# Chunk-selecting attention with a mixture of experts: score units of seven tiles, and another split of work in the first five pairs

## The chip, the cores and the metric

The kernel runs on one core of a Trainium2 chip, in one launch. The metric is the device time of one execution in microseconds (us). The engines are TensorE (PE; PEld is its weight load), VectorE (DVE), ScalarE (ACT) and GpSimd (POOL); SyncE (SP) only issues transfers here.

## The reference

The first half is attention in which each query sees only six chunks of 32 keys; the second half is a dense layer plus one routed expert of eight.

```python
# q, k, v: (4, 8, 768, 64); chunks of 32 keys
k_min, k_max = np.min(k_chunks, axis=3), np.max(k_chunks, axis=3)
ub = np.sum(np.maximum(q * k_min, q * k_max), axis=-1)       # per query and chunk
ub = np.where(causal, ub, -1e9)
top_chunks = np.argsort(ub, axis=-1)[..., -6:]
mask = sel & (pos[:, None] >= pos[None, :])                  # chosen chunk, and not later
scores = np.where(mask, q @ k.T / sqrt(64), -1e9)
attn_out = softmax(scores) @ v
x = attn_out.transpose(0, 2, 1, 3).reshape(3072, 512)
y_dense = np.maximum(x @ w1_dense, 0) @ w2_dense
# expert e = argmax(x @ w_gate), with its softmax weight
y_moe[rows of e] = gate_w * (np.maximum(x[rows of e] @ w1[e], 0) @ w2[e])
return y_dense + y_moe
```

## The kernel before

There are four batches of eight heads. The kernel takes two heads (g = 0 and 1) of a batch as one **pair**: the two heads' 64 features fill the 128 partitions. There are 16 pairs, four to a batch. A head has 768 positions, six tiles of 128. Scores are kept transposed (keys on the partitions, queries on the columns), so the causal half of a head is 21 tiles of 128 x 128.

**Preparation of a pair** is spread over the two pairs before it. `cast_qk` and `cast_v` turn the loaded fp32 values into fp16 on POOL. `prep_k` transposes the keys on PE into `pk`; ACT copies them to `kp`; DVE reduces `kp` to the largest and smallest key of each chunk (`ks`, line 502) and multiplies them by a sign mask into `kb` (line 505). `prep_kt` copies each half of `kp` into the key operand of its head, `kT[..][0]` and `kT[..][1]` (lines 509 and 510). `prep_q` transposes the queries into `pq`; ACT takes their relu into `qp` (line 520), DVE their negation into the query operands `rT` (lines 521 and 522). `prep_ub` makes the bounds `ub` on PE, and DVE finds the sixth largest of each query (`MAX8`, line 538) and flags the chunks below it (`fl`, line 540). `prep_s` transposes the flags on PE and DVE copies them into the free half of `rT` (lines 548 and 549). The free half of `kT` holds `exf`, a table of 30000 in the rows that belong to a key's chunk: so the score matmul itself adds the mask of unchosen chunks. `expand` copies `exf` into the six key operands once. There are three sets of `kT`, `rT` and `v16` (`NB` = 3), used in turn.

**A unit** is one score tile, `sp`, with its exp, `ex`. `scores` does the score matmuls (line 560) and the exp on ACT (line 564); where the unit lies on the diagonal, POOL zeroes the later keys in place (`affine_select`, line 566). `av` then multiplies `ex` with the values (line 579) into the output bank `op`, where a column of ones gives the row sum. After the last unit of a head `norm` takes the reciprocal (line 588) and writes the normalised rows to `xbig` (line 590). A pair has eleven units of up to four tiles (512 columns, one PSUM bank): five for each head, and one that holds the last two diagonal tiles of both. There are three score banks, two output banks (so one head's output can begin while the other's is normalised), and three banks for everything else. There are six `ex` tiles in SBUF.

**Order.** The loop runs over all 16 x 11 units. At step i it issues the scores of unit i + 2, then pieces of other work, then `av` of unit i - 1. The pieces stand at fixed units of a pair: flags of the next pair at unit 2, keys, queries, key operands and bounds of the pair after it at 4, 5, 7 and 9, casts and loads at units 0 and 7. An `issue_after` puts a piece behind the newest scores on PE and behind the exp before them on ACT. From the fifth pair on `fills` adds the work of the batch before: transposes of `xbig`, the gate, ranks, the scatter of rows to a table in DRAM (`place`), and 28 pieces of the dense layer (lines 387, 390, 399 and 404). `route_consts` makes the routing constants on POOL and writes empty rows to the table (line 187); it runs in the third pair. Expert weights are loaded by POOL's queue, one or two matrices a pair (line 206).

After the last pair the dense layer of the last batch and the expert blocks follow: rows are fetched from the table, multiplied with an expert's weights and added to the output by POOL's indirect transfers (line 744).

## Time and profile before

| what | value |
|---|---|
| median of three runs | 258.7 us (255.52 to 258.92) |
| the profiled execution | 257.3 us, span 255.5 us |
| mean granted TensorE clock | 0.994 |
| busy PE, DVE, ACT, POOL | 214.3, 179.8, 175.6, 159.6 us |
| first exp of the first pair | at 17.19 us |
| sixth pair begins, attention ends | at 55.13 us, at about 166.8 us |
| DMA packets | 75124, 50.12 MB |

The profile is of one execution. A row of the timeline gives the start from the begin of the span, the time that the instruction or merged run of instructions took, engine, line and operation; in brackets stands idle time ahead of it and what ended it. An instruction's own time includes its latency, so instructions that follow one another on an engine overlap a little: the time from start to start is what one costs an engine that is busy without a break. The busy share of PE is modelled from the starts of its matmuls.

### The profile page before, as it was taken

The numbers are of one execution on the slowest core, as the hardware profiler recorded it, in microseconds if no ns is written. First come the engines' busy times: TensorE is split into PE (matmuls) and PEld (weight loads), VectorE is DVE, ScalarE is ACT, GpSimd is POOL, SyncE is SP. The second block draws the span as 40 slices with busy tenths as digits, with TensorE's granted clock in tenths as the row PEclk, the third lists the DMA queues.
The fourth block names the chain that finished last, engine by engine and source line by source line (L and its number), as shares of the span: only waits on it lengthen the run. The fifth ranks groups of instructions, "written<-read, shape, count | busy, mean of one in ns | idle before, by whom it ended". The sixth has DMA issues, their size and how long they took to land. (4 is left out here: it accounts for less than half of the span.)

```text
span 255.5 us, 7236 instructions
## 1 busy us (share of the span) xinstructions
PE 214.3 (84%) x2547; PEld 141.4 (55%) x2547; DVE 179.8 (70%) x558; ACT 175.6 (69%) x332; POOL 159.6 (62%) x198
## 2 busy tenths in 40 slices
PE   1378969887989989999989988989579999999970
PEld 0256746655657676766567755655235555555530
DVE  6869989999989699898698896267233345555540
ACT  2799979877779887889789778924346465555530
POOL 4746998566177984379997235515755366776871
PEclk9999999999999999999999999999999999999997
DMA  7999999999889799979999934356979999885884
GB/s 179 262 266 236 213 225 264 228 210 209 215 146 323 122 293 247 232 164 212 321 213 270 198 76 129 106 152 193 249 164 206 232 220 186 144 140 70 120 122 92
DMA packets 75124, 50.12 MB, mean 196 GB/s; under 512 B 29648, under 2 KB 68176, under 8 KB 75088
## 3 DMA queue, kind: packets, MB, share of 16 engines
q1 hardware_dynamic: 59856, 30.33, 46.5%
q0 software_dynamic: 15232, 19.32, 46.1%
q8 instruction: 21, 0.34, 0.5%
q14 instruction: 15, 0.12, 0.2%
HBM read 41.93 MB, written 18.23 MB: 235 GB/s over the span
## 5 line engine op out<-in xcount | busy, mean ns | idle before, releaser
L564 ACT ACTIVATE ex<-sp 128x512 f16<-128x512 f32 (+1 forms) x176 | 91.3, 607 | 8.4 <-PE sp L560 4.1
L560 PE MATMUL sp<-rT,kT 128*128 128x128 f16 (+3 forms) x384 | 65.4, 260 | 3.9 <-ACT ex L564 2.4
L744 POOL DMA_INDIRECT out_dram<-yo,xg x28 | 43.2, 1545 | 23.5 <-DVE yo L743 17.2
L566 POOL TENSOR_SCALAR_AFFINE_SELECT ex<-ex 128x512 f16<-128x512 f16 x48 | 32.1, 683 | 39.7 <-ACT ex L564 28.9
L579 PE MATMUL op<-v,ex 128*128 128x65 f16 x672 | 48.5, 194 | 1.9 <-POOL ex L566 1.2
L579 PEld LDWEIGHTS <-ex 128*128 128x128 f16 x672 | 37.9, 98 | 20.3 <-POOL ex L566 5.7
L743 DVE TENSOR_SCALAR yo<-yp,xg 128x512 f32<-128x512 f32 x27 | 20.3, 751 | 24.0 <-PE yp L736 12.5
L370 POOL DMA_INDIRECT table<-xbig,slot x24 | 23.9, 997 | 19.1 <-issue 13.7
L560 PEld LDWEIGHTS <-kT 128*128 128x128 f16 x384 | 29.0, 98 | 8.5 <-issue 5.4
L718 ACT COPY ehT<-tp 128x512 f16<-128x512 f16 x28 | 16.4, 585 | 24.0 <-PE tp L716 17.3
L736 PE MATMUL yp<-we,ehT 128*128 x112 | 28.9, 379 | 2.1 <-ACT ys L404 1.3
L502 DVE TENSOR_REDUCE ks<-kp 128x24 f16<-128x768 f16 x30 | 27.3, 943 | 4.7 <-ACT kp L491 4.6
L387 PE MATMUL hp<-xT,wd 128*128 128x384 f16 x128 | 29.0, 325 | 1.5 <-DVE xT L258 1.3
L707 PE MATMUL hp<-we,exT 128*128 x112 | 29.1, 379 | 1.0 <-DVE exT L701 1.0
L399 PE MATMUL yp<-wd,hT 128*128 128x512 f16 x96 | 25.3, 379 | 2.8 <-issue 2.8
L710 ACT ACTIVATE eh<-hp 128x512 f16<-128x512 f32 x28 | 16.7, 597 | 12.4 <-PE hp L707 10.5
L701 DVE COPY exT<-tp 128x512 f16<-128x512 f16 x28 | 11.8, 423 | 15.7 <-PE tp L699 6.7
L390 ACT ACTIVATE hT<-hp 128x384 f16<-128x384 f32 x32 | 16.0, 502 | 8.8 <-PE hp L387 7.2
L491 ACT COPY kp<-pk 128x768 f16<-128x768 f16 x16 | 12.9, 806 | 9.1 <-PE pk L489 8.8
L404 ACT COPY ys<-yp 128x512 f32<-128x512 f32 x24 | 14.6, 607 | 6.4 <-PE yp L399 3.5
L590 DVE TENSOR_TENSOR xbig<-op,rs 128x384 f16<-128x384 f32 x32 | 17.5, 547 | 0.2
L736 PEld LDWEIGHTS <-ehT 128*128 128x128 f16 x112 | 10.1, 98 | 10.5 <-issue 1.7
(127 smaller groups left out, 383.1 us busy)
## 6 DMA issues: line engine op xcount, KB each, us to landing
we<-in_moe_w_dram POOLq DMA_DIRECT2D x16, 512.0 KB
kf<-in_k_dram SPq DMA_DIRECT2D x32, 192.0 KB
qf<-in_q_dram SPq DMA_DIRECT2D x32, 192.0 KB
vf<-in_v_dram SPq DMA_DIRECT2D x32, 192.0 KB
out_dram<-ys SPq DMA_DIRECT2D x48, 128.0 KB
xg<-table SPq DMA_DIRECT2D x28, 136.0 KB
table<-zt SPq DMA_DIRECT2D x9, 136.0 KB
wd<-in_moe_w_dense_dram POOLq DMA_DIRECT2D x2, 512.0 KB
```

Of the source, the lines that this page charges most:

```text
L370: sc = nc.gpsimd.indirect_dma_start(out=table, out_offset=bass.IndirectOffsetOnAxis(ap=keep["slot"][:, t : t + 1], axis=0), in_=xbig[b % 2 ...
L387: nc.tensor.matmul(hp, wd[:, ko, j * 128 : (j + 1) * 128], xT[:, ko, g * G * 128 : (g + 1) * G * 128], start=(ko == 0), stop=(ko == NK - 1))
L399: nc.tensor.matmul(yp, hold["h"][:, j, i * 128 : (i + 1) * 128], wd[:, NK + j], start=(j == 0), stop=(j == NK - 1))
L502: nc.vector.tensor_reduce(out=ks[:, i], in_=kp.rearrange("d (c w) -> d c w", w=32), op=op, axis=mybir.AxisListType.X)
L560: last = nc.tensor.matmul(sp[:, o : o + w], kT[p % NB][g][:, kt * 128 : (kt + 1) * 128], rT[p % NB][g][:, a * 128 : z * 128], start=(o == ...
L564: scored.append((last, nc.scalar.activation(ex[:, 0:o], sp[:, 0:o], AF.Exp, scale=-0.125)))
L566: latest["pool"] = nc.gpsimd.affine_select(out=ex, in_=ex, compare_op=ALU.is_ge, fill=0.0, base=0, pattern=[[0, 4], [1, 2], [2, 64]], chan ...
L579: nc.tensor.matmul(s["op", g][:, t * (D + 1) : (t + 1) * (D + 1)], ex[:, o : o + 128], v16[p % NB][:, g, kt, :], start=first, stop=(last_o ...
L707: nc.tensor.matmul(hp, s["xT"][:, ko], wef[:, bass.ds(offs[i] + ko * 512, 512)], start=(ko == 0), stop=(ko == NK - 1))
L736: nc.tensor.matmul(yp, s["hT"][:, j], wef[:, bass.ds(offs[i] + (NK + j) * 512, 512)], start=(j == 0), stop=(j == NK - 1))
L743: nc.vector.tensor_scalar(o, yp, gate, None, ALU.mult)
L744: sc = nc.gpsimd.indirect_dma_start(out=out, out_offset=to, in_=o, in_offset=None, bounds_check=N - 1, oob_is_err=False, compute_op=ALU.by ...
```

## The change

A head now has three units of seven tiles (896 columns over two PSUM banks): the first holds its six diagonal tiles and one other, so a pair has six units and two of them are masked. There are two score tiles of two banks, one output bank instead of two, and five `ex` tiles. `av` of a diagonal unit comes two steps after it instead of one, and the next unit's with it. The pieces stand in twelve slots of a pair, two a step.

In the first five pairs (`LEAN` = 5) the causal mask is added in PSUM by two matmuls of the identity with a constant tile, `later`, ahead of the score matmuls, and there is no `affine_select`. The keys of these pairs are copied by ACT straight into `kT[..][1]`. For the second to fifth pair POOL copies head 0's half from there to `kT[..][0]`, writes the `exf` rows over it, copies head 0's negated queries from `rT[..][1]` to `rT[..][0]`, and multiplies `kb`; DVE takes the relu in ACT's place. In the later pairs, and nearly so in the first, this preparation stays as it was, but `rT[..][1]` is now the whole negation and `rT[..][0]` its half. `route_consts` moves from the third to the fifth pair.

```diff
...
                                 fill=-60000.0, base=j, pattern=[[128, NT], [0, 2], [-32, NC]], channel_multiplier=2)
     for i in range(NB):
         nc.vector.memset(kT[i][0][64:128], 0.0)
-        nc.vector.memset(kT[i][1][0:64], 0.0)
         nc.vector.memset(v16[i][:, :, :, D : D + 1], 1.0)
 
     def members():
...
         nc.gpsimd.affine_select(out=exf[0:32], in_=exf[0:32], compare_op=ALU.is_ge, fill=0.0,
                                 base=31, pattern=[[-1, S]], channel_multiplier=32)
 
+
+    LEAN = 5
+    later = acst.tile([128, 128], HF)
+    nc.vector.memset(later, 0.0)
+    nc.gpsimd.affine_select(out=later, in_=later, compare_op=ALU.is_ge, fill=30000.0, base=0,
+                            pattern=[[1, NJ], [NJ, 64]], channel_multiplier=-1)
+
     def expand(i):
         nc.scalar.copy(kT[i][0][64:96, :], exf[0:32])
-        nc.scalar.copy(kT[i][1][0:32, :], exf[0:32])
 
 
     iom8 = const.tile([128, NT, E], FP)
...
 
     def of(g):
         return [
-            [(g, i, i, i + 1) for i in range(4)],
-            [(g, 0, 1, 5)],
-            [(g, 1, 2, 6)],
-            [(g, 2, 3, 6), (g, 4, 5, 6)],
-            [(g, 3, 4, 6), (g, 0, 5, 6)],
+            [(g, 0, 0, 1), (g, 1, 1, 2), (g, 2, 2, 3), (g, 3, 3, 4), (g, 5, 5, 6), (g, 4, 4, 6)],
+            [(g, 0, 1, 5), (g, 0, 5, 6), (g, 3, 4, 6)],
+            [(g, 1, 2, 6), (g, 2, 3, 6)],
         ]
 
-    units = of(0) + [[(g, i, i, i + 1) for g in range(2) for i in (4, 5)]] + of(1)
+    units = of(0) + of(1)
+    UW = 7 * 128
     NU = len(units)
     last_of = {}
     first_of = {}
     for u, pc in enumerate(units):
         for g, kt, a, z in pc:
-            first_of.setdefault(g, (u, kt))
             for t in range(a, z):
+                first_of.setdefault(g, (u, kt, t))
                 last_of[g, t] = (u, kt)
     done = [max(last_of[g, t][0] for t in range(NT)) for g in range(2)]
 
...
         at.setdefault(15, []).append(ranks)
         for t in range(NT):
             at.setdefault(18 + 4 * t, []).append(place(t))
-        U = HP * NU
+        U = 2 * HP * NU
         for n, f in enumerate(dense):
             at.setdefault(7 + n * (U - 9) // len(dense), []).append(f)
         return out_list, dense, ranks, [place(t) for t in range(NT)], at
...
     FIRST = 6
     with (
         tc.tile_pool(name="ahead", bufs=2) as ahead,
-        tc.tile_pool(name="aexp", bufs=6) as aexp,
-        tc.tile_pool(name="psc", bufs=3, space=bass.MemoryType.PSUM) as psc,
-        tc.tile_pool(name="pout", bufs=2, space=bass.MemoryType.PSUM) as pout,
+        tc.tile_pool(name="aexp", bufs=5) as aexp,
+        tc.tile_pool(name="psc", bufs=2, space=bass.MemoryType.PSUM) as psc,
+        tc.tile_pool(name="pout", bufs=1, space=bass.MemoryType.PSUM) as pout,
         tc.tile_pool(name="pprep", bufs=3, space=bass.MemoryType.PSUM) as pprep,
     ):
         def cast_qk(p):
...
             pk = pprep.tile([128, S], HF, name="pk", tag="pp")
             for t in range(NT):
                 nc.tensor.transpose(pk[:, t * 128 : (t + 1) * 128], s["k16"][:, t].rearrange("p g d -> p (g d)"), ident)
-            s["kp"] = kp = ahead.tile([128, S], HF, name="kp")
+            s["kp"] = kp = kT[p % NB][1] if p < LEAN else ahead.tile([128, S], HF, name="kp")
             nc.scalar.copy(kp.rearrange("d (T p j) -> d T p j", p=128, j=NJ),
                            pk.rearrange("d (T j p) -> d T p j", p=128, j=NJ))
             ks = ahead.tile([128, 2, NC], HF, name="ks")
...
                     nc.vector.tensor_reduce(out=ks[:, i], in_=kp.rearrange("d (c w) -> d c w", w=32), op=op,
                                             axis=mybir.AxisListType.X)
             s["kb"] = kb = ahead.tile([128, 2, 2, NC], HF, name="kb")
-            nc.vector.tensor_tensor(kb, ks.unsqueeze(2).to_broadcast([128, 2, 2, NC]), hmask, ALU.mult)
+            (nc.gpsimd if 0 < p < LEAN else nc.vector).tensor_tensor(kb, ks.unsqueeze(2).to_broadcast([128, 2, 2, NC]), hmask, ALU.mult)
 
         def prep_kt(p):
             kp = st[p]["kp"]
-            nc.vector.tensor_copy(kT[p % NB][0][0:64], kp[0:64])
-            nc.vector.tensor_copy(kT[p % NB][1][64:128], kp[64:128])
+            k0, k1 = kT[p % NB]
+            if p >= LEAN:
+                nc.vector.tensor_copy(k0[0:64], kp[0:64])
+                nc.vector.tensor_copy(k1[64:128], kp[64:128])
+            elif p:
+                nc.gpsimd.tensor_copy(k0[0:64], k1[0:64])
+                latest["pool"] = nc.gpsimd.tensor_copy(k1[0:32], exf[0:32])
+            else:
+                nc.vector.tensor_copy(k0[0:64], k1[0:64])
+                nc.scalar.copy(k1[0:32], exf[0:32])
 
         def prep_q(p):
             s = st[p]
...
                 nc.tensor.transpose(pqv[:, t // NJ, :, t % NJ], s["q16"][:, t].rearrange("p g d -> p (g d)"), ident)
             s["qp"] = qp = ahead.tile([128, S], HF, name="qp")
             r0, r1 = rT[p % NB]
-            nc.scalar.activation(qp, pq, AF.Relu)
-            nc.vector.tensor_single_scalar(r0, pq, -1.0, ALU.mult)
-            nc.vector.tensor_single_scalar(r1[64:128], pq[64:128], -1.0, ALU.mult)
+            if 0 < p < LEAN:
+                nc.vector.tensor_single_scalar(r1, pq, -1.0, ALU.mult)
+                nc.vector.tensor_single_scalar(qp, pq, 0.0, ALU.max)
+                latest["pool"] = nc.gpsimd.tensor_copy(r0[0:64], r1[0:64])
+            else:
+                nc.scalar.activation(qp, pq, AF.Relu)
+                nc.vector.tensor_single_scalar(r1, pq, -1.0, ALU.mult)
+                nc.vector.tensor_single_scalar(r0[0:64], pq[0:64], -1.0, ALU.mult)
 
         def prep_ub(p):
 
...
             nc.tensor.matmul(ub.rearrange("p t g c -> p (t g c)"), ident, cbias.rearrange("p t g c -> p (t g c)"),
                              start=True, stop=False, skip_group_check=True)
             for t in range(NT):
-                for n, (src, j) in enumerate(((s["qp"], 0), (s["qp"], 1), (rT[p % NB][0], 1))):
+                for n, (src, j) in enumerate(((s["qp"], 0), (s["qp"], 1), (rT[p % NB][1], 1))):
                     nc.tensor.matmul(ub[:, t].rearrange("p g c -> p (g c)"), src[:, t * 128 : (t + 1) * 128],
                                      s["kb"][:, j].rearrange("p g c -> p (g c)"),
                                      start=False, stop=(n == 2), skip_group_check=True)
...
 
         scored = []
 
+        def diagonal(u):
+            return units[u][0][1] == units[u][0][2]
+
         def scores(p, u):
             s = st[p]
             pc = units[u]
-            sp = psc.tile([128, 512], FP, name="sp")
+            sp = psc.tile([128, 1024], FP, name="sp")
+            o = 0
+            masked = p < LEAN and diagonal(u)
+            for n in (4, NT - 4) if masked else ():
+                nc.tensor.matmul(sp[:, o : o + n * 128].rearrange("p (n k) -> p n k", k=128), ident,
+                                 later.unsqueeze(1).to_broadcast([128, n, 128]),
+                                 start=True, stop=False, skip_group_check=True)
+                o = 512
             o = 0
             for g, kt, a, z in pc:
                 w = (z - a) * 128
                 last = nc.tensor.matmul(sp[:, o : o + w], kT[p % NB][g][:, kt * 128 : (kt + 1) * 128],
-                                 rT[p % NB][g][:, a * 128 : z * 128], start=(o == 0), stop=True, skip_group_check=True)
+                                 rT[p % NB][g][:, a * 128 : z * 128], start=(o % 512 == 0 and not masked), stop=True, skip_group_check=True)
                 o += w
-            ex = aexp.tile([128, 512], HF, name="ex")
-            scored.append((last, nc.scalar.activation(ex[:, 0:o], sp[:, 0:o], AF.Exp, scale=-0.125)))
-            if pc[0][1] == pc[0][2]:
-                latest["pool"] = nc.gpsimd.affine_select(out=ex, in_=ex, compare_op=ALU.is_ge, fill=0.0, base=0,
-                                        pattern=[[0, 4], [1, 2], [2, 64]], channel_multiplier=-1)
+            ex = aexp.tile([128, UW], HF, name="ex")
+            scored.append((last, nc.scalar.activation(ex, sp[:, 0:UW], AF.Exp, scale=-0.125)))
+            if diagonal(u) and not masked:
+                dg = ex[:, 0 : NT * 128]
+                latest["pool"] = nc.gpsimd.affine_select(out=dg, in_=dg, compare_op=ALU.is_ge, fill=0.0, base=0,
+                                        pattern=[[0, NT], [1, 2], [2, 64]], channel_multiplier=-1)
             s["ex", u] = ex
 
         def av(p, u):
...
             o = 0
             for g, kt, a, z in units[u]:
                 for t in range(a, z):
-                    first = first_of[g] == (u, kt) and t == a
+                    first = first_of[g] == (u, kt, t)
                     if first:
                         s["op", g] = pout.tile([128, 512], FP, name="op")
                     nc.tensor.matmul(s["op", g][:, t * (D + 1) : (t + 1) * (D + 1)], ex[:, o : o + 128],
...
 
         wq = [(e, w) for e in range(E) for w in range(2)]
         ahead_n = 2
-        LAG = 1
 
         def finish(p, u):
             av(p, u)
...
                     fills.update(batch_fills(p // HP)[-1])
 
         seq = [(p, u) for p in range(NP) for u in range(NU)]
+        due = {}
+        at = 0
+        for i, (p, u) in enumerate(seq):
+            at = max(at, i + (2 if diagonal(u) else 1))
+            due.setdefault(at, []).append((p, u))
         for i in range(ahead_n):
             scores(*seq[i])
-        for i, (p, u) in enumerate(seq):
+
+        def pieces(i, p, slot):
             n1 = p + 1 if p + 1 < NP else None
             n2 = p + 2 if p + 2 < NP else None
-            if i + ahead_n < len(seq):
-                scores(*seq[i + ahead_n])
 
             with tc.issue_after(scored[-1][0].ins), tc.issue_after(scored[-2][1].ins):
-                if u == 2 and n1 is not None:
+                if slot == 4 and n1 is not None:
                     prep_s(n1)
-                if u == 4 and n2 is not None:
+                if slot == 2 and n2 is not None:
                     prep_k(n2)
-                if u == 5 and n2 is not None:
+                if slot == 3 and n2 is not None:
                     prep_q(n2)
-                if u == 7 and n2 is not None:
+                if slot == 6 and n2 is not None:
                     prep_kt(n2)
-                if u == 9 and n2 is not None:
+                if slot == 7 and n2 is not None:
                     prep_ub(n2)
-                for f in fills.pop(i % (HP * NU) - LAG, ()):
+                for f in fills.pop(p % HP * 2 * NU + slot - 2, ()):
                     f()
-            if i >= LAG:
-                finish(*seq[i - LAG])
-            if u == 0 and n2 is not None:
+            if slot == 1 and n2 is not None:
                 with tc.issue_after(latest["pool"].ins):
                     cast_v(n2)
                 load(p + 4, "v")
                 if p == 1:
                     load_dense(st[n2]["cast"])
-                if p == 2:
+                if p == 4:
                     with tc.issue_after(st[n2]["cast"].ins):
                         route_consts()
                 for _ in range(2 if p >= 10 else 1):
                     if p > 1 and wq:
                         load_expert(*wq.pop(0), st[n2]["cast"])
-            if u == 7:
+            if slot == 6:
                 with tc.issue_after(latest["pool"].ins):
                     cast_qk(p + 3)
                 load(p + 5, "kq")
-            if p == NP - 2 and u == 8:
+            if p == NP - 2 and slot == 9:
                 load_rows(N1)
                 load_offs()
-            if p == NP - 1 and 3 <= u < 3 + FIRST:
-                fetch(u - 3)
-        for i in range(len(seq) - LAG, len(seq)):
-            finish(*seq[i])
+            if p == NP - 1 and 3 <= slot < 3 + FIRST:
+                fetch(slot - 3)
+
+        for i, (p, u) in enumerate(seq):
+            if i + ahead_n < len(seq):
+                scores(*seq[i + ahead_n])
+            pieces(i, p, 2 * u)
+            for d in due.pop(i, ()):
+                finish(*d)
+            pieces(i, p, 2 * u + 1)
+        for i in sorted(due):
+            for d in due[i]:
+                finish(*d)
         assert not wq
     att.close()
 
```

## The prediction

> **What bounds the kernel now.** I read the page first. It covers one execution whose own time was 257.3 us, with a span of 255.5 us, so 1.8 us lie around the span. The median of the runs is 258.7 us, 1.4 us above this execution. Everything below is summed against 257.3.
>
> ```profile
> PE 214.3 (84%) x2547; PEld 141.4 (55%) x2547; DVE 179.8 (70%) x558; ACT 175.6 (69%) x332; POOL 159.6 (62%) x198
> ```
>
> No engine is full over the whole span, so the shares must be read by stage. Next I cut the span at the first exp of a pair, in the view of busy time by stretches. Its columns are the stretch, its length, the busy time of PE, PEld, DVE, ACT and POOL with instruction counts, the granted clock, the DMA share and GB/s.
>
> ```profile
> 24.57:31.38 6.81, 6.28 (x104) 4.70 (x104) 6.36 (x24) 6.62 (x15) 6.13 (x9) 1.00 1.05 208
> 31.38:40.23 8.85, 6.57 (x107) 4.67 (x104) 7.82 (x26) 6.93 (x15) 8.39 (x24) 1.00 1.19 228
> 40.23:48.00 7.77, 6.31 (x107) 4.63 (x106) 7.58 (x25) 6.69 (x15) 5.09 (x7) 1.00 1.20 247
> 55.13:157.92 102.79, 93.53 (x1340) 67.58 (x1339) 90.93 (x310) 85.47 (x171) 65.55 (x86) 1.00 0.98 215
> 166.82:255.46 88.64, 75.16 (x553) 41.09 (x553) 38.23 (x85) 40.25 (x71) 51.13 (x36) 0.98 0.83 163
> ```
>
> The first three rows are the second, third and fourth pair, which carry no dense or routing work. DVE is busy 7.58 of 7.77 us in the fourth: those pairs are DVE's. The next row is the sixth to fifteenth pair, with dense work in between; there DVE has 90.93 of 102.79 us, PE 93.53 and ACT 85.47, so four engines press together. The last row is the expert stage, 88.6 us that the edit does not touch. I count it as unchanged.
>
> One full DVE cycle of an unfilled pair, from one pair's chunk reductions to the next, is in DVE's timeline (start, us, engine, line).
>
> ```profile
> 40.03 1.79 DVE L502 TENSOR_REDUCE ks<-kp 128x24 f16<-128x768 f16 x2
> 41.75 0.54 DVE L521 TENSOR_SCALAR rT<-pq 128x768 f16<-128x768 f16 x1
> 42.21 0.19 DVE L505 TENSOR_TENSOR kb<-ks,hmask 128x96 f16<-128x96 f16 x1
> 42.44 0.56 DVE L522 TENSOR_SCALAR rT<-pq 64x768 f16<-64x768 f16 x1
> 43.01 0.35 DVE L509 COPY kT<-kp 64x768 f16<-64x768 f16 x1
> 43.38 0.76 DVE L510 COPY kT<-kp 64x768 f16<-64x768 f16 x1
> ...
> 47.80 1.79 DVE L502 TENSOR_REDUCE ks<-kp 128x24 f16<-128x768 f16 x2
> ...
> 53.35 0.55 DVE L590 TENSOR_TENSOR xbig<-op,rs 128x384 f16<-128x384 f32 x1
> ```
>
> The cycle is 47.80 - 40.03 = 7.77 us and no row in it shows idle time. Everything taken off DVE here shortens the pair, until something else is as long.
>
> **The change part by part.** *Preparation of the second to fifth pair.* DVE loses kb (0.19), the half negation (0.56) and both key copies (0.35 and 0.76), 1.86 us; it gains the relu of the queries, for which I use the whole negation from the same PSUM tile (0.54). Net 1.3 us a cycle, four cycles. On GpSimd appear three copies of 768 columns and the small product. Its nearest rows are these.
>
> ```profile
> 6.83 0.81 POOL L138 TENSOR_SCALAR_AFFINE_SELECT exf<-exf 32x768 f16<-32x768 f16 x1
> 32.75 0.82 POOL L483 CAST v<-vf 128x768 f16<-128x768 f32 x1
> 33.51 0.45 POOL L171 MEMSET xbig<- 128x192 f16 x2
> ...
> 36.34 0.79 POOL L206 DMA_DIRECT2D we<-in_moe_w_dram  x1
> 37.15 1.31 POOL L566 TENSOR_SCALAR_AFFINE_SELECT ex<-ex 128x512 f16<-128x512 f16 x2
> ...
> 43.26 1.40 POOL L566 TENSOR_SCALAR_AFFINE_SELECT ex<-ex 128x512 f16<-128x512 f16 x2 [0.21 <-ACT ex L564]
> ```
>
> A copy is bounded by 0.45/2 = 0.22 (a memset of 192 columns) and 0.82 (a cast of 768); I take 0.82, the same column count. The product of 96 columns lies between 0.2, as on DVE, and 0.65, a select of 512 columns; I take 0.3. Together 2.8 us a pair, while the three selects of a pair (2.0 us by these rows) go. In the second pair GpSimd, 6.13 us busy, would come to 6.9 of 6.81: nothing is won there. The copies also wait for DVE (the halves overwritten by the expansion rows must have been reduced first), and the casts of the pair after next are queued behind them, and behind those the loads that reuse the cast's buffer. In the other three cycles the full gain is 3.9 us. The floor is PE: 6.31 busy plus the mask matmuls (next) is about 6.95, which leaves 0.8 a cycle, 2.4 in all. I take **-3.2**.
>
> *Masks by matmul in pairs 0 to 4.* Each diagonal unit gets a 512- and a 256-column matmul. Six 512-column matmuls with their last latency took 1.46 us.
>
> ```profile
> 185.05 1.46 PE L399 MATMUL yp<-wd,hT 128*128 128x512 f16 x6
> ```
>
> Less one latency of 0.38 that is 0.22 each, so 0.33 a unit and 0.65 a pair. PE is not the bound of these pairs, so DVE's cycle covers it: nothing. Without that cover it would be 5 x 0.65 = 3.3 us.
>
> *Routing constants.* Their block runs from 33.51 to 36.34, 2.8 us in POOL's queue in the third pair, ahead of the select at 37.15 and the key cast; the table's empty rows also leave SP later. That pair took 8.85 us against 7.77 for the next. In the fifth pair no select is queued behind the block, and by my count only the gate step, a pair later, needs it. Bounds 0 and 8.85 - 7.77 = 1.1; I take **-1.0**.
>
> *Longer exps.* Eleven exps a pair become six of 896 columns.
>
> ```profile
> 17.19 2.04 ACT L564 ACTIVATE ex<-sp 128x512 f16<-128x512 f32 x4
> ...
> 38.83 0.80 ACT L491 COPY kp<-pk 128x768 f16<-128x768 f16 x1 [1.15 <-PE pk L489]
> 39.53 0.82 ACT L520 ACTIVATE qp<-pq 128x768 f16<-128x768 f16 x1
> 40.23 5.29 ACT L564 ACTIVATE ex<-sp 128x512 f16<-128x512 f32 x11
> ```
>
> From start to start 768 columns take 39.53 - 38.83 = 0.70. The run of eleven (5376 columns, 5.29) less the run of four (2048 columns, 2.04) leaves seven with 3328 columns in 3.25. With a fixed part a and b a column, a + 768 b = 0.70 and 7a + 3328 b = 3.25 give b = 0.00081 and a = 0.08. Five fixed parts fewer are 0.4 us a pair. The columns stay. In the early pairs DVE hides this; in the eleven later pairs it is at most 4.4 us, at least nothing (other engines hold the pair); I take **-2.0**, about half.
>
> *Select and its wait.* In later pairs two selects of 768 columns (0.81 each by the row at 6.83, at most 1.0 scaled from 512) replace three of 512. The output matmuls of a diagonal unit now come two units later. The list of waits for 55 to 148 us, where not DVE alone is the bound, has what PE's weight loads lose there (us in all, times, longest).
>
> ```profile
> PEld L579 <- POOL ex L566: 1.4, 5, 0.5
> ```
>
> Earlier waits of this kind lie under DVE's cycle. Bounds 0 and 1.4; I take **-1.2**.
>
> *One output bank, two score tiles of two banks.* Two score tiles hold 14 tiles of 128 columns against 12 in three banks before, so ACT's lead is no shorter. The output bank is new: the first output matmul of a head now waits for the normalisation of the head before. Behind it in PE's queue stand the next scores, the transposes and the dense matmuls; ACT waits for the scores.
>
> ```profile
> 48.25 0.26 PE L579 MATMUL op<-v,ex 128*128 128x65 f16 x3
> ...
> 49.40 0.30 PE L579 MATMUL op<-v,ex 128*128 128x65 f16 x4
> 126.16 0.29 PE L579 MATMUL op<-v,ex 128*128 128x65 f16 x4
> ...
> 129.67 0.54 DVE L590 TENSOR_TENSOR xbig<-op,rs 128x384 f16<-128x384 f32 x1
> ```
>
> Counting 42 output matmuls a pair, a head ends at 48.51 and its normalisation at 53.90 (the row at 53.35 above): 5.4 us late, while the next head began on the other bank at 49.40. In a filled pair the same lag runs from about 126.4 to 130.2, 3.8 us. The new order leaves two units between the heads, a third of a pair: 2.6 us at 7.77 and 3.4 at 10.3. But DVE is late only because PE may run ahead; once PE waits, the normalisation is taken up sooner, and DVE lives on its queue meanwhile. Bounds 0 and the rival below; I take **+1.5**.
>
> *Start.* One of two key copies, three memsets and half of the six expansion copies go; most is off the chain to the first exp at 17.19, which loses one DVE copy: **-0.4** (0 to -0.8).
>
> Sum: -3.2 - 1.0 - 2.0 - 1.2 + 1.5 - 0.4 = -6.3, so **251.0 us**. With every term at its best and no bank wait it is 257.3 - 3.9 - 1.1 - 4.4 - 1.4 - 0.8 = 245.7; with the early gain at its floor, the others at nothing and the bank at 1.5 it is 256.4. The likeliest case's own range is 246 to 256.
>
> **The rivals.** *The output bank decides: slower.* Place: each change of head. It decides once the normalisation ends later than two units after the head's last matmul. An unfilled pair: 5.4 - 2.6 = 2.8 us, less PE's idle 7.77 - 6.31 = 1.5, is 1.3 for four pairs, 5.2 us, and the gains of the early pairs (-3.2, -1.0) are gone. A filled pair: 3.8 - 3.4 = 0.4 at each of 22 heads, 8.8 us, of which half may be hidden. 257.3 - 0.4 - 2.0 - 1.2 + 5.2 + 4.4 = **263.3**. For it: the lags are measured. Against it: DVE catches up while PE stands.
>
> *The gain is larger: 246.8.* Over the ten filled pairs DVE idles 102.79 - 90.93 = 11.9 us. If these idles come from the many small hand-overs between ACT, POOL and PE, half of them go: -5.9 in place of -2.0 - 1.2 + 1.5 = -1.7. For it: fewer, longer units and a later use of masked ones. Against it: 0.4 us a pair is all that a row shows.
>
> *The loads hold the pairs: 255.2.* The DMA share is 1.05 to 1.20 in the early pairs. If keys and values come no sooner, what those pairs save (3.2 + 1.0) is waited for. Against it: no cast waits for a load between 30 and 60 us, and the filled pairs let the loads catch up.
>
> *Moving copies from DVE to GpSimd gives nothing: 254.2.* The same copy took 0.35 at 43.01 and 0.76 at 43.38, after POOL's select had begun at 43.26. If the moved copies slow DVE as much as they free it, the -3.2 is lost. [...] Against it: what stays on DVE in these pairs reads PSUM or is a reduction, and the reductions took 1.79 at 40.03 and at 47.80 alike.
>
> **How the numbers follow.** Forecast 0.46 (0.42 of it over 2% faster, below 253.5 us), larger gain 0.17, loads 0.09, nothing from GpSimd 0.05, output bank 0.23. Two per cent of 258.7 is 5.2 us, about what a measurement of this kernel can tell from no change. Faster 0.42 + 0.17 = 0.59; within 2% 0.04 + 0.09 + 0.05 = 0.18; slower 0.23. The range goes from 244.5, a little under the larger gain, to 264, which takes in the middle of the bank's case.
>
> **What would show it.** Right: the DVE cycle of the first four pairs at 6.5 to 7 us; exps of 896 columns about 0.8 us from start to start; no select before the sixth pair; the constants' block in the fifth pair with nothing waiting behind it; the first output matmul of a head seldom waiting for L590's successor. Wrong: waits of output matmuls for the normalisation of more than 5 us in all, ACT waiting for scores behind them, casts waiting for loads in the first six pairs, or GpSimd over 95% busy in the early pairs.

## The result and the profile after

The changed kernel took 269.0 us (median of four runs, 267.57 to 270.63), the kernel before 258.8 us on the same chip. The ratio is 1.044, interval 1.0319 to 1.0561: **slower**, where 251.0 us was forecast and 264 us was the upper end of the range. The profiled execution took 269.22 us with a span of 267.4 us, 11.9 us more than the 255.5 us of before.

The kernel before had medians from 252.7 to 258.8 us in the comparisons of this study. So each run below is given as its ratio to the kernel before, run beside it. These ratios leave out executions that took over 1.5% more than the fastest of the same kernel. The comparisons ran on different chips (before: 252.7 us on chip 3, 257.3 us on chip 7), so lengths of stages are compared on one chip where a run there allows it.

The busy line of the page of after stands first. DVE and ACT are 8 us less busy than before, POOL 0.5 us less, and PE 3 us more.

```profile
PE 217.4 (81%) x2535; PEld 144.1 (54%) x2535; DVE 171.8 (64%) x543; ACT 167.4 (63%) x246; POOL 159.1 (60%) x189
```

Next is the view by stretches of after, with the same columns as in the prediction, cut at the first exp of a pair: the second to fifth pair, the sixth to fifteenth, and the expert stage.

```profile
24.73:32.75 8.02, 6.42 (x107) 4.90 (x106) 7.03 (x22) 5.87 (x8) 6.75 (x10) 1.00 0.91 178
32.75:40.61 7.86, 6.52 (x107) 4.96 (x106) 6.52 (x23) 5.77 (x7) 6.51 (x10) 1.00 1.17 225
40.61:47.51 6.90, 6.01 (x88) 4.47 (x87) 4.99 (x17) 6.48 (x9) 3.62 (x6) 1.00 0.92 200
47.51:58.52 11.01, 7.90 (x115) 5.89 (x114) 9.84 (x31) 6.48 (x9) 6.31 (x21) 0.93 1.01 207
58.52:164.07 105.55, 90.94 (x1304) 65.49 (x1303) 85.82 (x304) 81.72 (x118) 64.00 (x76) 0.99 0.98 205
173.51:267.40 93.89, 77.93 (x557) 42.90 (x556) 38.42 (x85) 40.23 (x71) 50.48 (x36) 0.93 0.78 154
```

The reader is to see two losses. The attention ends at 173.51 us against 166.82 us, 6.7 us late. The expert stage, whose code the diff doesn't touch, takes 93.89 us against 88.64 us, at a granted clock of 0.93 against 0.98: 5.3 us. Together they are the 11.9 us. In the third pair (the second row) DVE is busy 6.52 of 7.86 us: its work did shrink as forecast, but now something else holds the pair.

**First loss: the flags.** This row is from the list of waits of after (engine, line, released by, total us, times, longest).

```profile
ACT ex L591 <- PE sp L587: 21.4, 21, 2.3
```

In the same list of before it is 4.1 us.

```profile
ACT ex L564 <- PE sp L560: 4.1, 9, 1.3
```

So ACT waits for scores 21 times. PE itself stands 8 times, 3.0 us in all, until the flags of those scores are copied; in e1 below, where they are early, no such wait is listed. ACT's, DVE's and PE's timelines of after show one such wait, at the start of the third pair.

```profile
24.73 3.66 ACT L591 ACTIVATE ex<-sp 128x896 f16<-128x896 f32 x4 [1.97 <-PE sp L587]
28.29 0.79 ACT L495 COPY kT<-pk 128x768 f16<-128x768 f16 x1
28.97 1.75 ACT L591 ACTIVATE ex<-sp 128x896 f16<-128x896 f32 x2
32.74 2.53 ACT L591 ACTIVATE ex<-sp 128x896 f16<-128x896 f32 x3 [2.03 <-PE sp L587]
```
```profile
28.56 0.55 DVE L534 TENSOR_SCALAR qp<-pq 128x768 f16<-128x768 f16 x1
29.19 1.81 DVE L506 TENSOR_REDUCE ks<-kT 128x24 f16<-128x768 f16 x2
31.03 0.56 DVE L565 COPY rT<-ps 64x768 f16<-64x768 f16 x1
31.62 0.55 DVE L566 COPY rT<-ps 64x768 f16<-64x768 f16 x1
```
```profile
29.95 0.48 PE L580 MATMUL sp<-later,ident 128*128 128x512 f16 x2
31.65 0.33 PE L587 MATMUL sp<-rT,kT 128*128 128x128 f16 x3 [1.21 <-DVE rT L565]
```

The chain is read backwards. The exp at 32.74 waits for the scores, which PE starts at 31.65 when the flags of that pair are in `rT` (L565). DVE copies the flags only at 31.03, behind the relu of the queries (28.56) and two key reductions (29.19), both work of the pair after it. The reductions can't begin before ACT has copied the keys (28.29 to 29.08), and that copy stands behind four exps. Before, `prep_s` stood at unit 2 of eleven, ahead of `prep_k` at 4 and `prep_q` at 5. In the change it stands in slot 4 of twelve, behind `prep_k` in slot 2 and `prep_q` in slot 3. Its readers, the next pair's first scores, are issued two steps ahead of that pair.

**Second loss: the first rows of the expert stage.** The chain that ended last, of after, passes through these pieces (start, us, what).

```profile
172.84 2.44 DMA table<-xbig,slot
175.30 2.17 DMA xg<-table
177.52 0.62 PE tp L737 x4
```

PE's timeline of after at that place, then of before at the same place, and a stretch of after (its granted clock is the 0.50).

```profile
177.52 0.61 PE L737 MATMUL tp<-ident,xg 128*128 128x128 f16 x4 [3.03 <-DMA xg<-table]
...
180.73 0.63 PE L745 MATMUL hp<-we,exT 128*128 x1
181.16 0.63 PE L261 MATMUL tp<-ident,xbig 128*128 128x128 f16 x4
```
```profile
167.32 1.02 PE L707 MATMUL hp<-we,exT 128*128 x4 [0.95 <-DVE exT L701]
...
169.30 0.38 PE L707 MATMUL hp<-we,exT 128*128 x1
169.51 0.39 PE L257 MATMUL tp<-ident,xbig 128*128 128x128 f16 x4
```
```profile
176.60:183.40 6.80, 5.79 (x54) 4.33 (x55) 2.97 (x7) 0.60 (x1) 0.00 (x0) 0.50 0.80 215
```

Rows are fetched from the table only after the last scatter into it that stands ahead of them: in the chain above the scatter takes 2.44 us from 172.84, and the fetch starts at 175.30. In the new slots that scatter stands at slot 4 of the last pair with a single fetch (slot 3) ahead of it; before, it stood at unit 6 with the fetches of units 3, 4 and 5 ahead. So the second block's rows come late and PE stands 3.03 us. The granted clock is 0.50 for 6.8 us, 5.9 of them behind the wait: the same matmul takes 0.63 us instead of 0.38. Counted from the end of attention, PE takes up the third block's rows at 10.9 us, against 5.7 in before: that is the loss. Of the 5.3 us, 3.0 are the wait; the other 2.3 fit an estimate from the 5.9 us at a clock of 0.50: half of them, 2.9, at most.

### The profile page after: what moved, and what is told of

Same layout as the page of the kernel before. It is cut to its first block, busy times and chain, and to the rows that moved or that the text cites. A ratio compares the mean times of both kernels' runs of the same rounds, so it can differ in the third digit from the quotient of the medians.

```text
span 267.4 us, 7086 instructions
## 1 busy us (share of the span) xinstructions
PE 217.4 (81%) x2535; PEld 144.1 (54%) x2535; DVE 171.8 (64%) x543; ACT 167.4 (63%) x246; POOL 159.1 (60%) x189
## 5 line engine op out<-in xcount | busy, mean ns | idle before, releaser
L591 ACT ACTIVATE ex<-sp 128x896 f16<-128x896 f32 x96 | 86.0, 928 | 26.9 <-PE sp L587 21.4
L587 PE MATMUL sp<-rT,kT 128*128 128x128 f16 (+3 forms) x352 | 53.7, 273 | 2.9 <-DVE rT L565 1.6
L594 POOL TENSOR_SCALAR_AFFINE_SELECT ex<-ex 128x768 f16<-128x768 f16 x22 | 20.4, 927 | 33.4 <-ACT ex L591 26.6
L781 DVE TENSOR_SCALAR yo<-yp,xg 128x512 f32<-128x512 f32 x27 | 20.2, 750 | 22.9 <-PE yp L774 11.1
L607 PEld LDWEIGHTS <-ex 128*128 128x128 f16 x672 | 28.6, 98 | 11.6 <-issue 4.1
L587 PEld LDWEIGHTS <-kT 128*128 128x128 f16 x352 | 26.6, 100 | 14.2 <-issue 3.1
L607 PE MATMUL op<-v,ex 128*128 128x65 f16 x672 | 32.2, 193 | 2.2 <-DVE xbig L618 2.1
L403 PE MATMUL yp<-wd,hT 128*128 128x512 f16 x96 | 26.7, 379 | 4.8 <-issue 3.0
L748 ACT ACTIVATE eh<-hp 128x512 f16<-128x512 f32 x28 | 16.7, 598 | 18.3 <-PE hp L745 16.2
L739 DVE COPY exT<-tp 128x512 f16<-128x512 f16 x28 | 11.9, 424 | 22.3 <-PE tp L737 12.8
L506 DVE TENSOR_REDUCE ks<-kp 128x24 f16<-128x768 f16 x22 | 19.9, 947 | 7.6 <-ACT kp L495 7.5
L487 POOL CAST v<-vf 128x768 f16<-128x768 f32 x16 | 13.3, 830 | 11.7 <-PE op L607 8.9
L555 DVE MAX8 m<-ub 128x8 f32<-128x8 f32 (+4 forms) x160 | 15.6, 164 | 1.5 <-PE ub L549 1.5
```

The costliest lines, as they stand in the source:

```text
L403: nc.tensor.matmul(yp, hold["h"][:, j, i * 128 : (i + 1) * 128], wd[:, NK + j], start=(j == 0), stop=(j == NK - 1))
L506: nc.vector.tensor_reduce(out=ks[:, i], in_=kp.rearrange("d (c w) -> d c w", w=32), op=op, axis=mybir.AxisListType.X)
L587: last = nc.tensor.matmul(sp[:, o : o + w], kT[p % NB][g][:, kt * 128 : (kt + 1) * 128], rT[p % NB][g][:, a * 128 : z * 128], start=(o % 5 ...
L591: scored.append((last, nc.scalar.activation(ex, sp[:, 0:UW], AF.Exp, scale=-0.125)))
L594: latest["pool"] = nc.gpsimd.affine_select(out=dg, in_=dg, compare_op=ALU.is_ge, fill=0.0, base=0, pattern=[[0, NT], [1, 2], [2, 64]], cha ...
L607: nc.tensor.matmul(s["op", g][:, t * (D + 1) : (t + 1) * (D + 1)], ex[:, o : o + 128], v16[p % NB][:, g, kt, :], start=first, stop=(last_o ...
```

## The experiments

**The two pieces put back, one at a time, on one chip.**

```diff
 # e1_flags_first
-                if slot == 4 and n1 is not None:    # prep_s
+                if slot == 2 and n1 is not None:
 # e4_fetch_earlier
-            if p == NP - 1 and 3 <= slot < 3 + FIRST:
-                fetch(slot - 3)
+            if p == NP - 1 and 1 <= slot < 1 + FIRST:
+                fetch(slot - 1)
```

> The changed kernel, with the flags of the next pair (prep_s) moved from slot 4 to slot 2, where they stand ahead of the keys of the pair after it. Theory A (flags too late): in the changed kernel DVE copies the flags behind two reductions of 0.9 us each, and the first scores of a pair wait for them; ACT idles about 2 us at the start of each early pair. With the flags first this idle time should fall below 0.8 us a pair and the attention part should end 4 to 9 us sooner: 260 to 265 us. Theory B (the single output bank sets the head change): flags are not what is waited for, the normalisation still ends late: 267 to 270 us. Theory C (tail alone): no more than 1 us gained in the attention part.

Measured: no interval is on record. The two executions within the limit took 253.52 and 254.61 us, against a median of 252.4 us for the kernel before: about 1.007. (The expectations in us for e1 to e4 were made for a chip on which the kernel before takes 258.8 us, so they are to be read as ratios: 260 to 265 us is 1.005 to 1.024.) The attention ends at 164.1 us; in e4 below, on the same chip and with late flags, at 169.4. ACT's waits for scores are 8.2 us, against 20.2 in e4.

```profile
ACT ex L591 <- PE sp L587: 8.2, 16, 1.5
```

The expert stage still has its gap of 3.07 us, and the matmul behind it (0.38 us in before) takes 0.63 us, as in after.

> The changed kernel, with the first expert rows of the last pair fetched from slot 1 on instead of slot 3, so that three fetches again stand ahead of the last scatter of the third batch's rows. Theory C: TensorE's 3.0 us wait for the second block's rows at the start of the expert part goes: 265 to 267 us, attention part unchanged. Against it: the rows are not what is waited for, or the wait comes back one block later: 268 to 270 us.

Measured: 1.022, interval 1.0126 to 1.0314. The list of waits and the view by stretches of this kernel:

```profile
ACT ex L591 <- PE sp L587: 20.2, 23, 2.0
```
```profile
169.37:255.40 86.03, 74.82 (x553) 41.53 (x553) 37.93 (x85) 40.19 (x71) 51.13 (x36) 0.97 0.83 168
```

The expert stage takes 86.03 us, the fetched rows keep PE 0.25 us, and the same matmul takes 0.38 us again, while ACT's waits for scores stay. The third block's rows come 5.7 us behind the end of attention again. That is 5.2 of the 7.9 us between this stage and the 93.89 us of after. Most of the rest is a stop of PE ahead of a dense matmul, 2.76 us in the profile of before and 2.68 in that of after, which this one has not, so it is no work of the edit. Each edit removes its own loss and leaves the other.

**Both together, and the change itself beside them.** e5 has both edits; e6 is the change unaltered.

> The changed kernel with both repairs: flags of the next pair at slot 2, fetches of the last pair from slot 1. If the two causes (A, late flags; C, late fetches and the half clock behind their wait) are separate, their gains add: about 5% under the changed kernel, 0.98 to 1.0 of the kernel before, with the attention part at or under 148 us and the expert part under 88 us. If they overlap (the fetches only hid behind the late flags): 1.005 to 1.02.

> The changed kernel as it is, beside the others on the same chip: 1.035 to 1.055 of the kernel before, with TensorE's wait of 3 us for the second block's rows and half the clock for some 7 us behind it.

Measured: e5 0.9959, interval 0.9906 to 1.0011; e6 1.0351, interval 1.0216 to 1.0486. Putting two pieces elsewhere takes back about 4%: 1.022 to 0.9959 for the flags (2.6%), the rest, 1.3%, for the fetches. e1 agrees: 1.007 is 2.8% under e6 and 1.1% over e5. That is the whole loss. It doesn't bring the forecast gain: the repaired kernel is level with before.

**The late flags in the kernel before.**

```diff
 # e12_before_flags_late: the kernel before
-                if u == 2 and n1 is not None:       # prep_s
+                if u == 6 and n1 is not None:
```

> The kernel before, with the flags of the next pair at unit 6 instead of unit 2, so behind the keys and queries of the pair after it as in the changed kernel; nothing else. Theory A: the first scores of a pair wait for the flags, as in the changed kernel: 4 to 10 us slower (1.015 to 1.04), ACT idle at the start of pairs. If three units of 0.7 us are still enough, or the late flags hurt only with long units: within 2 us.

Measured: 1.0468, interval 1.0391 to 1.0546. Its list of waits shows the mark of the change:

```profile
ACT ex L564 <- PE sp L560: 24.8, 22, 3.2
```

So the order of one piece alone, with no new unit, no lighter preparation and two output banks, costs as much as the whole change did, more than was expected. Its size can't be carried over to the change, though. Its runs had a mean granted clock of 0.959 to 0.964, against 0.980 to 0.994 in the runs of before beside them; for the change it was 0.963 to 0.979 with the loss in its expert stage, and 0.99 in the attention part of after (17.00 to 173.51). What the lower clock adds in e12 was not measured apart. And the flags are issued three units of 0.7 us ahead of their first reader here, against two of 1.3 us in the change. For the change itself e1, e4 and e5 give the size.

**The lighter preparation left out** (`LEAN = 0`, with the memset and the copy that it had made needless), from the change (e3) and from the repaired kernel (e7).

> The changed kernel with LEAN = 0: masks by GpSimd's select and keys, queries and kb prepared by ACT and DVE in all pairs, as in the later pairs (the clearing of the second key operand and its expansion rows are put back); units, banks, order and the place of the routing constants stay. If the split of the first five pairs costs time (GpSimd's queue delays casts and loads): 264 to 267 us, with loads waited for less. If it gains what was forecast (3 us): 271 to 274 us. Theory A expects the early pairs to stay at about 8 us or more, since the late flags stay.

> Both repairs, and LEAN = 0: masks by select and preparation by ACT and DVE in all pairs. If the split of the first five pairs gains what the forecast's terms say once the order is repaired (DVE's cycle 1.3 us shorter in three or four pairs): 3 to 5 us slower than with both repairs alone. If GpSimd's queue takes back what DVE saves: within 1.5 us of it.

Measured: e3 1.0458, interval 1.0367 to 1.055, where 264 to 267 us would be 1.020 to 1.032 and 271 to 274 us 1.047 to 1.059. The change itself gave 1.044, and 1.0351 in e6, so the totals don't tell whether the lighter preparation gains. The profiles do: on the same chip the sixth pair begins at 61.74 us in e3 and at 57.94 us in e4, whose first five pairs are the change's own. Without the lighter preparation the first exp is 1.0 us later and the first five pairs are 2.8 us longer, even with the flags late. e7 1.0153, interval 1.0038 to 1.0267, against 0.9959 for e5. The second to fifth pair of e7, then of e5, by stretches:

```profile
24.60:32.53 7.93, 5.50 (x96) 4.10 (x94) 7.66 (x24) 6.47 (x10) 6.60 (x8) 1.00 1.02 194
32.53:41.02 8.49, 5.80 (x101) 4.53 (x101) 7.48 (x25) 6.34 (x10) 4.91 (x6) 1.00 1.11 218
41.02:49.83 8.81, 5.80 (x101) 4.54 (x101) 7.52 (x25) 6.49 (x10) 4.89 (x6) 1.00 1.05 215
49.83:58.85 9.02, 6.53 (x112) 5.10 (x112) 8.26 (x27) 6.49 (x10) 5.49 (x20) 1.00 0.86 198
```
```profile
23.26:29.93 6.67, 6.30 (x109) 5.05 (x108) 6.11 (x22) 5.90 (x8) 5.56 (x9) 1.00 0.47 114
29.93:37.26 7.33, 6.76 (x103) 4.81 (x103) 6.45 (x22) 6.09 (x8) 7.06 (x11) 1.00 1.16 187
37.26:45.06 7.80, 7.18 (x117) 5.31 (x117) 6.77 (x22) 6.68 (x9) 5.73 (x8) 1.00 1.20 235
45.06:53.26 8.20, 6.50 (x111) 4.97 (x108) 7.97 (x25) 6.60 (x10) 2.26 (x3) 1.00 1.16 249
```

The first five pairs take 41.6 us in e7 and 37.1 us in e5, so the lighter preparation gains 4.5 us there. (In e1, which has the same first five pairs as e5, they take 37.3 us.) But before they took 37.9 us: without it the rest of the change (units, banks, exp tiles, order) costs 3.7 us there. The waits of e7 from 24.6 to 58.9 us say where.

```profile
PE sp L589 <- ACT ex L593: 6.7, 12, 1.0
ACT ex L593 <- PE op L609: 6.4, 3, 2.1
...
PE op L609 <- DVE xbig L620: 3.2, 3, 1.1
```

Three times the output matmuls wait for a normalisation, and ACT stands two us each time for the output matmuls. That is the output bank's wait as the rival had it. In e5 no such row is left in those pairs: DVE has time to normalise.

**One output bank in the kernel before** (`pout` with one buffer instead of two).

> The kernel before, with one output bank in place of two and nothing else (a PSUM bank stays unused). Theory B: every head waits for the normalisation of the one before, so the attention part grows by 6 to 15 us: 265 to 274 us. Theory A: with the old order the flags are early, and DVE takes up the normalisation sooner once PE stands: 258 to 263 us.

Measured: 1.0424, interval 1.033 to 1.0518, in the range of theory B (1.024 to 1.059). In the early pairs its exps wait for output matmuls.

```profile
ACT ex L564 <- PE op L579: 10.1, 4, 3.5
```

**A second output bank in the repaired kernel.** Here it comes from the three shared banks: e9 takes one of these away and gives it to nobody, and e8 gives it to the output.

```diff
 # e8_both_two_out: both lines; e9_both_two_shared: the second alone
-        tc.tile_pool(name="pout", bufs=1, space=bass.MemoryType.PSUM) as pout,
-        tc.tile_pool(name="pprep", bufs=3, space=bass.MemoryType.PSUM) as pprep,
+        tc.tile_pool(name="pout", bufs=2, space=bass.MemoryType.PSUM) as pout,
+        tc.tile_pool(name="pprep", bufs=2, space=bass.MemoryType.PSUM) as pprep,
```

> Both repairs, two output banks, and two banks instead of three for everything else. Theory B: the wait of a head's first output matmul for the normalisation goes, and the attention part ends 3 us or more sooner, unless the third shared bank was worth more. Theory A alone: no gain from the second output bank, and the missing shared bank delays transposes, bounds and dense tiles: 2 to 8 us slower than with both repairs alone.

> Both repairs, one output bank, and two shared banks instead of three (one bank stays unused). Against the run with two output banks and two shared ones it differs in the second output bank alone. Theory B for the new order: without the second output bank it is 2 us or more slower than that run (267 us or more, 1.05 of the kernel before). If the new order of the output matmuls hides the head change: within 2 us of it (1.035 to 1.05), and the whole loss of that run was the third shared bank.

Measured: e8 1.0411, interval 1.0293 to 1.0529; e9 1.0354, interval 1.0239 to 1.0469. The third shared bank is worth 4%, and the second output bank nothing that can be told beside two shared ones. This pair alone doesn't clear the output bank: in e9 exps wait 12.9 us for output matmuls, in e8 that wait is gone and they wait 12.0 us for scores instead of 2.8. The list of waits of e5, with one output bank and three shared ones, does:

```profile
PE op L607 <- DVE xbig L618: 0.3, 1, 0.3
```

So the rival's mechanism exists (e2, e7), but it isn't what made the change slower.

**The routing constants back in the third pair** of the repaired kernel (`p == 4` becomes `p == 2`).

> Both repairs, with the routing constants put back to the third pair. The forecast gave their move 1.0 us. If that is right, the third pair grows from 7.3 to about 8.3 us and the fifth shrinks; the time goes to 0.995 to 1.005 of the kernel before. If the casts behind the block are what matters (loads issued 2.8 us later while the transfers are full): 1.5 to 4 us slower than with both repairs.

Measured: 1.0006, interval 0.9961 to 1.0051, against 0.9959 for e5 on another chip. The first five pairs take 38.1 us against 37.1. The forecast -1.0 is there in size, but not where it was expected: the third pair stays at 7.33 us and the fourth grows (8.93 against 7.80). The totals don't resolve it.

**Other orders of the pieces, and the loads.** e11 is e4 with the flags in slot 0, keys 1, queries 2, key operands 7, bounds 8. e13 is e11, e14 is e5 and e15 is the kernel before, each with the expert weights asked for later.

```diff
-                    for _ in range(2 if p >= 10 else 1):
+                    for _ in range(3 if p >= 12 else 1):
```

> The changed kernel with the earlier fetches and all preparation of a pair spread anew: flags at slot 0, keys at 1, queries at 2, key operands and bounds only behind the first head's normalisation (slots 7 and 8). If the normalisation of the first head is late because DVE still works on keys and queries ahead of it, its lag falls from 3 to 5 us to about 1 us in the filled pairs and the time to 0.97 to 0.985 of the kernel before. If the lag is hidden anyway, or loads hold the pairs: 0.99 to 1.01.

> Keys, queries and bounds spread anew and earlier fetches, and expert weights loaded one a pair up to the twelfth pair and three in the thirteenth and fourteenth. If the loads of the last pairs hold it (the fourteenth pair took 18.5 us, behind TensorE's wait of 6.4 us): that pair comes down to 10 to 12 us, 0.965 to 0.985 of the kernel before. If not: 1.01 to 1.03 as without this edit, or the weights are late for the experts.

> Both repairs, and the same later weights. If the loads took what was missing to the forecast: 0.975 to 0.99 of the kernel before, the fourteenth pair at 10.7 us in each run. If they did not: 0.99 to 1.005.

> The kernel before with the later weights and nothing else. Its last values landed 2.4 us ahead of their cast, so the weights should not hold it: 0.99 to 1.01 of the kernel before. If it gains over 1%, the gain of the other two is not the change's.

Measured: e11 1.0242 (1.0153 to 1.0331), e13 0.9957 (0.9918 to 0.9996), e14 1.0216 (1.0108 to 1.0323), e15 1.0042 (1.0002 to 1.0083). In e11 the fourteenth pair took 18.47 us, with the query cast waiting for its load:

```profile
140.65 0.83 POOL L482 CAST q<-qf 128x768 f16<-128x768 f32 x1 [4.50 <-DMA qf<-in_q_dram]
```

With the weights later (e13) that pair takes 10.56 us. So in this order the weight transfers and the pair's loads collided, though neither total is in its expected range. The profile of e5 shows a milder case: its fourteenth pair takes 14.56 us, against 10.69 in e1, behind a value cast that waits for its load.

```profile
142.35 0.82 POOL L487 CAST v<-vf 128x768 f16<-128x768 f32 x1 [5.57 <-DMA vf<-in_v_dram]
```

In e14 the same edit doesn't help, against both expectations: the seventh, eighth, eleventh and twelfth pair take 13.81, 12.03, 13.48 and 11.95 us, against 12.36, 9.23, 12.36 and 9.79 in e5, and the first two lie before the edit acts. That isn't explained. The change itself, unaltered, took 12.04, 11.03, 11.98 and 10.31 us for these pairs in after and 11.49, 10.26, 10.77 and 10.16 us in e6, so up to 1.2 us of such a difference comes without any edit.

**The lighter preparation in more pairs, and a sixth exp tile.** e16 is e5 with `LEAN = 9`; e17 is e5 and e18 is e7 with six `ex` tiles instead of five.

> The changed kernel with flags in slot 2, fetches from slot 1, and LEAN = 9: the lighter preparation and the masks by matmul hold for pairs 0 to 8. Theory: LEAN pays where DVE carries the pair and PE has room, 1 us a pair, so the ninth pair (no dense pieces) may gain 0 to 1 us, but in the sixth to eighth, where PE is the fullest engine, two mask matmuls a pair (0.65 us) are added: together 0 to +2 us, ratio to before 0.996 to 1.004. Rival: lighter DVE and no select in a filled pair are worth as much as in the early ones, 1 us a pair: -4 us, ratio about 0.98.

> The changed kernel with flags in slot 2, fetches from slot 1, and six ex tiles instead of five. Theory: with the lighter preparation no wait of an exp for the output matmuls is left in the early pairs and the filled pairs are bound elsewhere: no difference, ratio to before 0.993 to 0.999. Rival: the sixth ex tile lets ACT run a unit further ahead in the filled pairs: -2 us or more, ratio 0.988 or less.

> The same repaired order with LEAN = 0 and six ex tiles (five gave 1.0153). In the early pairs there, exps waited 2.15 us a pair for output matmuls to give back an ex tile, while those output matmuls had waited 1.05 us for the normalisation. Theory: the single output bank under a DVE that is full all through decides; a sixth ex tile changes little, the first five pairs take 40.5 to 42 us in all (41.6 with five tiles), ratio 1.010 to 1.016. Rival: the number of ex tiles decides, then the first five pairs come back to the 37.9 us of before, ratio about 1.000.

Measured: e16 1.0337 (1.023 to 1.0443), e17 1.01 (1.0059 to 1.0141), e18 1.0204 (1.0066 to 1.0341). e16 fell outside both expectations: the seventh and eighth pair take 16.69 and 13.07 us, against 13.05 and 11.97 in e17 on the same chip, so in filled pairs the lighter preparation costs. In e18 the first five pairs take 40.5 us, against 41.6 with five tiles and 37.9 before, and the wait stays:

```profile
ACT ex L593 <- PE op L609: 5.7, 3, 1.9
```

A sixth tile gives back 1.1 of the 3.7 us, as its theory said; the rest fits the output bank, which no run here shows by itself. e17 agrees with neither expectation. Its instructions on ACT also stand in another order, and its seventh and eighth pair (13.05 and 11.97 us) are as long as those of e14. None of the runs is clearly faster than before: e5 and e13, at 0.996, come nearest.

## Why the prediction was wrong

**The moved piece that was not costed.** The part on the change went through every edit but one: the new slots of the pieces. No term priced that `prep_s` now follows `prep_k` and `prep_q` on DVE, so neither the sum nor a rival held the late flags. The runs show that the late flags cost 2.6% (e4 against e5) to 2.8% (e6 against e1) in the change, and 4.7% in the old units (e12). The prediction looked at instructions and their durations, and left their order aside.

**"The expert stage, 88.6 us that the edit does not touch."** It took 93.9 us in place of 88.6. The fetches that feed it stand in the attention's slots, and they had moved behind the last scatter. e4 takes this back. The same step (what each moved piece has ahead of it in its queue) would have shown it.

**The early pairs, -3.2.** The gain exists, and is larger than the term and its bound of 3.9: 4.5 us between e7 and e5, and e7's waits fit a reason: a DVE that is full also normalises late. It was an exchange, though: the output bank was given +1.5 in the whole kernel, while the rest of the change costs 3.7 us in the first five pairs alone where DVE is full (e7). Net the repaired early pairs gain 37.9 - 37.1 = 0.8 us and the start another 1.0 us (first exp at 16.2 against 17.19; -0.4 was forecast). GpSimd's copies cost what was taken for them, and its small product 0.36 us (0.3 was taken), by its timeline in after:

```profile
31.09 0.36 POOL L509 TENSOR_TENSOR kb<-ks,hmask 128x96 f16<-128x96 f16 x1 [0.37 <-DVE ks L506]
31.40 0.81 POOL L518 COPY kT<-kT 64x768 f16<-64x768 f16 x1
```

The rival by which moving copies to GpSimd gives nothing falls with e7, and what stayed on DVE wasn't slowed: two key reductions take 1.81 us in after and 1.79 in before. The flag copies, which read PSUM, take 0.56 and 0.55 us in after (at 31.03 and 31.62), with POOL's copy at 31.40 beside them, and as long in before (at 46.27 and 46.86), where POOL did nothing. That reading PSUM is what spares them was not shown, and no run moves the copies alone.

**Longer exps, -2.0, and the select, -1.2.** One exp costs what was worked out: by the rows at 28.97 and 32.74 a third one adds 2.53 - 1.75 = 0.78 us, where the forecast's fixed part and columns make 0.81. But the filled pairs gained little or nothing from it: the sixth to thirteenth take 81.7 us before, 80.5 in e5, 80.9 in e7 and 84.3 in e10. Such differences are within what one kernel shows by itself: the change took 86.2 us there in after and 82.7 in e6. The select's wait did go: PE's weight loads lost 5.7 us to it over the whole span of before and lose 0.2 in after, without a gain that can be seen. So neither ACT's instruction count nor the select held the filled pairs. Of the two readings "at least nothing (other engines hold the pair)" and 4.4 us, the lower bound was near the truth.

The reading "four engines press together" counted one too many: in its row POOL is busy 65.55 of 102.79 us.

**Routing constants, -1.0:** right in size by the profiles (e10), a pair later than argued.

**The rivals.** "The output bank decides" came nearest in its number, 263.3 us, but by luck. Its wait of output matmuls for the normalisation, in the list of waits of after, is under the 5 us that the prediction named as its mark, and in e5 it is 0.3 us.

```profile
PE op L607 <- DVE xbig L618: 2.1, 6, 0.7
```

"The loads hold the pairs": in after's fourth pair casts do wait, which the prediction named as a sign.

```profile
43.12 0.83 POOL L480 CAST k<-kf 128x768 f16<-128x768 f32 x1 [1.35 <-DMA kf<-in_k_dram]
45.88 0.83 POOL L482 CAST q<-qf 128x768 f16<-128x768 f32 x1 [1.93 <-DMA qf<-in_q_dram]
```

But that pair took only 6.9 us, the shortest of the five. In the fifth, which took 11.0 us against 8.2 in e5, casts wait 0.41 and 0.50 us, while ACT stands 2.2 us for an output matmul and 2.3 us for scores. So in the early pairs loads delay casts, and no row shows that they hold a pair. "The gain is larger" is refuted by the filled pairs.

**What stays open:** why the seventh, eighth, eleventh and twelfth pair are 2 to 3 us longer in some of the repaired kernels (e10 in part, e14, e17) than in e5, and with that whether e5's 0.996, measured on one chip, would hold on others or under other small edits. The output bank and the units of seven tiles were changed apart only in e2, in the old units; their shares in the 3.7 us are argued from e7's waits.

## What to carry to other kernels

When a change regroups a loop, list for every moved piece what now stands ahead of it on each engine's queue and when its first reader is issued; here two positions in an order cost 4%, more than all the priced terms. A stage whose code isn't touched can still lose (5.3 us here), if its first loads are issued from the stage before. And a gain on the busiest engine counts only after the waits on it are gone: the same lighter preparation was worth 2.8 us in its pairs with the flags late and 4.5 us with them early.

## What the hardware showed that was not expected

The wait of 3 us at PE cost more than itself: behind gaps of 3.03 to 3.07 us (after, e1, e6) four transposes of fetched rows took 0.61 us, and behind 0.25 us (e4) 0.40; in after the granted clock was 0.50 for 6.8 us there. The length of a gap alone didn't decide it in these profiles. A shorter gap in after, 1.67 us, was followed by 3.4 us at a granted clock of 0.50, while behind one of 2.68 us there, and one of 2.76 us in before, it was 1.00.

```profile
56.90 0.45 PE L261 MATMUL tp<-ident,xbig 128*128 128x128 f16 x4 [1.67 <-DVE rT L539]
...
194.57 0.39 PE L403 MATMUL yp<-wd,hT 128*128 128x512 f16 x1 [2.68 <-issue]
```
```profile
57.10:60.50 3.40, 3.25 (x37) 2.53 (x35) 2.99 (x9) 0.92 (x1) 0.92 (x1) 0.50 1.18 221
```
